# Attention and expert routing on one core: transposes as single passes, the sink columns' exponentials on their own path, transfers in halves of 64 partitions

## The chip, the cores and the metric

The kernel runs on one core of a Trainium2 chip. The metric is the device time of one execution in microseconds (us). A run is one execution; times of several runs are given by their median.

## The reference, cut to what matters

Two steps follow each other. First an attention in which every query sees the 4 first keys (the sinks) and the 128 keys up to itself; then a mixture of experts that assigns each of the 3072 tokens to one of 8 experts of equal capacity and sends it through that expert's two matrices.

```python
batch, n_heads, seq, head_dim = 4, 8, 768, 64          # n_sink, window = 4, 128
scores = (q @ k.transpose(0,1,3,2)) / sqrt(64)
keep   = (pos[None,:] < 4) | ((rel >= 0) & (rel < 128))
a      = softmax(where(keep, scores, -1e9))             # + 1e-9 in the denominator
x      = (a @ v).transpose(0,2,1,3).reshape(3072, 512)
logits = x @ w_gate                                     # 8 experts
# largest logits first, each token to one expert, at most 384 tokens per expert
out[mask] = maximum(x[mask] @ w1[e], 0) @ w2[e]         # expert by expert
```

## The kernel before, in words

The work of the attention is cut into 24 chunks: 4 batches times 6 blocks of 128 queries, all 8 heads at once. A chunk c goes through these steps; the two numbers behind a name are its two halves, four heads each.

- The loads `ldk`, `ldq` (lines 30 and 31, four chunks ahead) and `lv` (line 32) bring keys, queries and values of 256 KB each; SP issues them and the store `xo` in one order.
- `qs` (line 74, POOL) scales the queries.
- `QK0`, `QK1` (line 83, PE): scores into PSUM, as products of 64x64 parts, 8 per half. Partitions hold the queries of two 64-row parts, and the columns hold 64 keys of the block before, 4 sinks and 128 keys of the block.
- `cp`, `mx` (lines 89 to 94, DVE): masking and the negated maximum.
- `e0` to `e3` (line 99, ACT): the exponentials of 132 columns, with their sum.
- `T0`, `T1` (line 107, PE): P transposed by products with the identity, 16 per half, each 64x64. `pe` (line 108, ACT) copies them to SBUF as `PT`; `A`, `B` (lines 110 and 111, POOL) split the two diagonal parts into the keys of this block and of the one before.
- `ss` (line 114, ACT), `Ts` (line 118, PE), `pS` (line 119, ACT): the 4 sink columns of P are copied out and transposed on their own.
- `AV0`, `AV1` (line 129, PE): P times the values; `ae` (line 132, DVE) copies the result out.
- `X` (lines 136 and 138, PE): the sinks' values are added, and heads are brought into rows, 64 columns of x and 8 of the router's logits for each head; `ra`, `r` (lines 130 and 131, DVE) make one over the sum, `xe` (line 140, DVE) multiplies by it, `lm` (line 142, DVE) adds the logits up over heads.
- `xo` (line 143, SP): x to DRAM, in pieces of 64 numbers.

Products in 32-bit floats are issued to PE as two passes, each with a load of its weights of its own; so one of them appears in the trace as two MATMUL and two LDWEIGHTS instructions. A transpose in PE's transpose mode is one of each, as at line 667.

The order in which the steps of several chunks are interleaved on the five engines is computed when the kernel is built: `schedule` walks the steps with a cost for each (`table`), rings of buffers (`buffers`: four PSUM buffers `p` are shared by QK, T, Ts, AV and X), waits between engines, and a priority per step (`OFF`).

When the last chunk's logits are there, the second part starts: the routing by a search for thresholds (lines 519 to 569), the gathers of x by token (line 659), their transposes (line 667), the loads of the experts' matrices `raw`, and their products (lines 680 and 692). Its weights wait for the routing's first result.

Of the kernel before, what the change touches and what calls it, by code (L numbers as in the profile page):

```python
# [11 lines left out]
W=132  # L12
# [3 lines left out]
def attention(ctx,tc,qd,kd,vd,vs,ud,iwd,ident,idn,x_dram,L,side={}):  # L16
# [34 lines left out]
    G.memset(mf[0:64],1); G.memset(mf[64:128],0); G.memset(mf[64:128,4:8],1); G.memset(m0[0:64,0:4],1)  # L51
# [23 lines left out]
    def op_QK(c,g):  # L75

        i=c%NB; q=qs[c%NQ]; sp=T('p',c,f'QK{g}')
        k0=(i-1)*W+4 if i else -128
        for u in range(2):
            for s in range(2):  # L80
                for f in range(2):
                    p,o=half(s),half(f); a=0 if i else 64 if f else 128
                    PE.matmul(sp[o,s,196*u+a:196*u+196],q[p,g+2*u,o],kk[p,g+2*u,k0+64*f+a:k0+64*f+196],start=True,stop=True)  # L83
    def scores(c,g): return T('p',c,f'QK{g}')[:,:,0:392].rearrange("p s (u n)->p s u n",u=2)
    def op_cp(c,g):

# [26 lines left out]
    def op_ss(c):  # L113
# [16 lines left out]
    def op_ra(c): V.tensor_scalar(T('r',c),T('sm',c),1e-9,None,op0=OP.add)  # L130
# [23 lines left out]
def layouts(q,k,v,wg,n_sink=4):  # L154

    pairs=lambda x: x.reshape(B,HP,2,64,NB,-1).transpose(2,3,0,4,1,5).reshape(128,B,NB,-1)
    qT=q.transpose(0,1,3,2); kT=k.transpose(0,1,3,2)
    qd=pairs(qT.reshape(B,H,64,NB,128))
    sk=np.broadcast_to(kT[:,:,:,None,:4],(B,H,64,NB,4))
    kd=pairs(np.concatenate([sk,kT.reshape(B,H,64,NB,128)],-1))  # L160
# [12 lines left out]
    return {n:np.ascontiguousarray(a) for n,a in dict(qd=qd,kd=kd,vd=vd,vs=vs,ud=ud,iwd=iwd,ident=np.eye(128,dtype=np.float32)).items()}  # L173
# [5 lines left out]
def table(cfg):  # L179
    o={}  # L180
    def add(k,e,c,deps,alloc=()): o[k]=(e,c,deps)
# [29 lines left out]
    add('xe','V',680,[('X',0),('r',0)])  # L211
# [21 lines left out]
def schedule(cfg,off,T,nb=NC,dl={}):
# [34 lines left out]
    et=collections.defaultdict(float); et['E']=3700.0; mode=['n']; out=[]; ld=[]; fills=[]; dq=[0.0]  # L268
# [28 lines left out]
    while len(out)<total:  # L297
# [49 lines left out]
SWITCH=dict(nr=90,rn=200)  # L347
# [6 lines left out]
OFF={'A0': 18335, 'A1': 52415, 'AV0': 14908, 'AV1': 84106, 'B0': 47216, 'B1': 7783, 'QK0': 2872, 'QK1': 4297, 'T0': 8328, 'T1': -8153, 'Ts': 15650, 'U': -22652, 'Uc': -13081, 'cp0': -10470, 'cp1': 78107, 'e0': 58010, 'e1': 95573, 'e2': 687, 'e3': 927, 'fi': 95598, 'lm': -9483, 'mx0': 14597, 'mx1': -49747, 'pS': 60593, 'pe0': 61206, 'pe1': -9424, 'pr0': 95367, 'pr1': -19606, 'pr10': -47988, 'pr11': 79834, 'pr12': 60010, 'pr13': -8724, 'pr14': 3651, 'pr15': 2764, 'pr2': 75294, 'pr3': -25455, 'pr4': 59901, 'pr5': -70, 'pr6': 12471, 'pr7': 98043, 'pr8': -8311, 'pr9': 6044, 'qs': 50785, 'r': 61220, 'ra': -6513, 'ss': 79894, 'um': 11705, 'xe': -10955, 'xo': -20341, 'zs': -5463, 'pr16': -102190, 'ae': -9891, 'X': -32988}  # L354
# [374 lines left out]
def attention_general(ctx,tc,qd,kd,vd,iwd,ident,idn,x_dram,L,n_sink,window):  # L729
# [10 lines left out]
    for b in range(B):  # L740
# [6 lines left out]
        for i in range(NB):  # L747
# [74 lines left out]
```

## Time and profile before

| what | us |
|---|---|
| three runs, median (lowest to highest) | 545.25 (541.69 to 548.64) |
| the profiled execution | 545.01 |
| its span | 543.3 |

Between the span and the profiled execution's own time lie 1.7 us. In the profile PE is TensorE's matrix products and PEld its loads of weights, DVE VectorE, ACT ScalarE, POOL GpSimd, SP SyncE; SPq and PEq stand for the sequencers of these. A wait is named by what ended it; "issue" means that the engine waited for nothing that the profile shows. PEclk is the granted clock of TensorE as a share of full speed.

### The profile page before, as it was taken

To read this page: it belongs to the slowest core of one execution; us is meant where nothing else is said; L and a number is where in the kernel's file an instruction comes from. 1 tells how busy PE (TensorE), PEld (TensorE's weight loads), DVE (VectorE), ACT (ScalarE), POOL (GpSimd) and SP (SyncE) were. 2 spreads that over 40 slices of the span, in tenths; PEclk is the share of its full clock that TensorE was granted. 3 is DMA by queue.
4 is the path that set the end of the run, shared out by engine and by line. 5 is a ranking of instruction groups with operands and counts; after the bars stand their busy time and mean duration, and the time that the engine had idled before them with its cause. 6 is when DMAs were issued, how large, how long until landed. Compare 5 with 4: busy or idle time off the path is not lost.

```text
span 543.3 us, 16624 instructions
## 1 busy us (share of the span) xinstructions
PE 468.9 (86%) x6873; PEld 400.3 (74%) x6873; DVE 352.7 (65%) x1040; ACT 237.2 (44%) x690; POOL 174.0 (32%) x231
## 2 busy tenths in 40 slices
PE   7777776877777478898999998999999989999995
PEld 4666765776676246886987886887888889988983
DVE  3666656667667677789698796787798674452210
ACT  3966766776773014335253254163154244352210
POOL 6867766768543020016031021103130212001001
PEclk9999999999999569899899998999999989999999
DMA  7656645555322137056082191272290595101001
GB/s 237 201 171 167 167 140 159 160 160 167 83 74 51 32 117 246 8 187 220 21 303 85 61 326 40 74 276 79 79 329 21 180 373 184 58 21 54 25 6 53
DMA packets 75085, 73.23 MB, mean 135 GB/s; under 512 B 28033, under 2 KB 57601, under 8 KB 75009
## 3 DMA queue, kind: packets, MB, share of 16 engines
q1 hardware_dynamic: 71168, 59.58, 35.3%
q0 software_dynamic: 3840, 12.59, 6.4%
q8 instruction: 54, 0.88, 0.7%
q14 instruction: 23, 0.18, 0.1%
HBM read 59.57 MB, written 12.58 MB: 133 GB/s over the span
## 4 chain that ended last, share of the span: by engine, by line
PE 57%; DMA 15%; DVE 12%; issue 10%; ACT 2%; POOL 2%; SPq 1%; POOLq 0%; ACTq 0%; DVEq 0%
PE ph L680 16%; PE py L692 15%; DMA raw<-w 12%; PE pp L129 6%; PE pp L83 5%; PE pp L107 5%; PE pp L138 2%; PE pp L136 2%; PE pr L543 2%; DVE wl L654 2%; DVE cmp L473 2%; PE pt L667 1%; DMA xg<-x_dram,idx 1%; DVE hl L684 1%; DMA us<-ud 1%
## 5 line engine op out<-in xcount | busy, mean ns | idle before, releaser
L652 ACT ACTIVATE wh<-raw 128x1024 fp32r<-128x1024 f32 x64 | 67.8, 1060 | 76.9 <-DMA raw<-w 38.9
L680 PE MATMUL ph<-xh,wh 128*128 128x384 f32 x256 | 92.3, 360 | 4.0 <-DVE hl L684 4.0
L654 DVE TENSOR_TENSOR wl<-raw,wh 128x1024 fp32r<-128x1024 f32 x64 | 77.7, 1220 | 23.2 <-ACT wh L652 22.9
L680 PE MATMUL ph<-xl,wh 128*128 128x384 f32 x256 | 88.1, 344 | 0.0
L680 PE MATMUL ph<-xh,wl 128*128 128x384 f32 x256 | 88.0, 344 | 0.0
L692 PE MATMUL py<-wh,hh 128*128 128x512 f32 x192 | 79.9, 416 | 2.2 <-ACT yo L695 2.2
L697 POOL DMA_INDIRECT out<-yo,idx x24 | 26.7, 1114 | 166.9 <-ACT yo L695 113.4
L659 POOL DMA_INDIRECT xg<-x_dram,idx x24 | 33.3, 1389 | 139.5 <-issue 49.5
L692 PE MATMUL py<-wh,hl 128*128 128x512 f32 x192 | 75.9, 395 | 0.0
L692 PE MATMUL py<-wl,hh 128*128 128x512 f32 x192 | 75.8, 395 | 0.0
L99 ACT ACTIVATE P<-pp,nmx 128x132 f32<-128x132 f32 x192 | 69.0, 372 | 7.9 <-DVE nmx L94 6.6
L683 ACT ACTIVATE hh<-ph 128x384 fp32r<-128x384 f32 x64 | 31.2, 488 | 82.3 <-PE ph L680 61.7
L684 DVE SCALAR_TENSOR_TENSOR hl<-ph,hh 128x384 fp32r<-128x384 f32 x64 | 35.3, 553 | 39.7 <-ACT hh L683 39.1
L107 PE MATMUL pp<-idt,P 64*64 64x64 f32 x1536 | 39.6, 226 | 23.5 <-issue 23.5
L680 PEld LDWEIGHTS ph<-xh,wh 128*128 128x128 f32 x256 | 50.2, 196 | 7.1 <-DVE hl L684 5.1
L107 PEld LDWEIGHTS pp<-idt,P 64*64 64x64 f32 x1536 | 35.0, 140 | 24.0 <-issue 23.5
L110 POOL TENSOR_TENSOR E<-PT,me 128x256 f32<-128x256 f32 x48 | 35.7, 744 | 49.2 <-ACT PT L108 48.6
L680 PEld LDWEIGHTS ph<-xl,wh 128*128 128x128 f32 x256 | 49.6, 194 | 2.0
L680 PEld LDWEIGHTS ph<-xh,wl 128*128 128x128 f32 x256 | 49.6, 194 | 0.0
L83 PE MATMUL pp<-kk,q 64*64 64x196 f32 (+2 forms) x768 | 44.5, 327 | 4.8 <-issue 3.5
L108 ACT ACTIVATE PT<-pp 128x512 f32<-128x512 f32 x48 | 28.6, 597 | 33.1 <-PE pp L107 32.9
L692 PEld LDWEIGHTS py<-wh,hh 128*128 128x128 f32 x192 | 36.9, 192 | 7.6 <-ACT yo L695 2.6
(157 smaller groups left out, 863.8 us busy)
## 6 DMA issues: line engine op xcount, KB each, us to landing
raw<-w SPq DMA_DIRECT2D x64, 512.0 KB, 8.3
v<-vd SPq DMA_DIRECT2D x24, 256.0 KB, 3.8
x_dram<-xt SPq DMA_DIRECT2D x24, 256.0 KB, 3.1
kk<-kd SPq DMA_DIRECT2D x23, 264.0 KB, 4.3
q<-qd SPq DMA_DIRECT2D x23, 256.0 KB, 4.9
xg<-x_dram,idx POOLq DMA_INDIRECT x24, 5.8
out<-yo,idx POOLq DMA_INDIRECT x24, 2.8
us<-ud SPq DMA_DIRECT2D x1, 288.0 KB, 4.8
```

What stands on the lines that cost most here:

```text
L83: PE.matmul(sp[o,s,196*u+a:196*u+196],q[p,g+2*u,o],kk[p,g+2*u,k0+64*f+a:k0+64*f+196],start=True,stop=True)
L99: A.activation(T('P',c)[:,h,:],sp[:,s,u,64:196],AF.Exp,bias=T('nmx',c)[:,b:b+1],scale=1.0,accum_out=T('sm',c)[:,h:h+1])
L107: for u in range(2): PE.matmul(t[half(u),s,128*x+64*l:128*x+64*l+64],T('P',c)[half(s),2*(g+2*u)+x,a:a+64],idn[half(s),half(s)],start=True, ...
L110: def op_A(c,g): G.tensor_tensor(T('E',c)[:,2*g:2*g+2],diag(c,g),me[:,None].to_broadcast([128,2,2,64]),OP.mult)
L129: PE.matmul(av[half(s),u,a:a+64*n],T('v',c-w)[half(u),256*l+64*x:256*l+64*x+64],m.rearrange("p a n->p (a n)"),start=g==0 and n==2 and w==0 ...
L652: g.add('A',947,lambda wh=wh,raw=raw: nc.scalar.activation(wh,raw,AF.Copy),[f'raw{q}'],[f'wh{s}'],f'H{k}.{j}',f'W{k}')
L654: g.add(e,{'V':1135,'P':2303}[e],lambda wh=wh,wl=wl,raw=raw,e=e: (nc.vector if e=='V' else nc.gpsimd).tensor_tensor(wl,raw,wh.bitcast(F32) ...
L659: g.add('P',1038,lambda t=t: nc.gpsimd.indirect_dma_start(out=self.xg[t],out_offset=None,in_=self.x_dram,in_offset=bass.IndirectOffsetOnAx ...
L680: nc.tensor.matmul(p[:,0:CAP],x[:,c,:],y[:,c,:],start=c==0 and i==0,stop=c==3 and i==2)
L683: g.add('A',371,lambda f=f,p=p: nc.scalar.activation(self.hh[:,f,:],p[:,0:CAP],AF.Relu),ps,[f'hh{f}'],f'hh{k}.{f}',f'H{k}')
L684: g.add('V',469,lambda f=f,p=p: nc.vector.scalar_tensor_tensor(self.hl[:,f,:],p[:,0:CAP],0.0,self.hh[:,f,:].bitcast(F32),op0=OP.max,op1=OP ...
L692: nc.tensor.matmul(p,x[:,f,ts],w,start=f==0 and i==0,stop=f==7 and i==2)
```

## The change

1. **Transposes in one pass.** P is stored as [4 pairs][2 halves of keys][2 heads][64], so that 64 rows by 128 columns can be transposed at once in PE's transpose mode; T is 8 such instructions per half in place of 16 products of 64x64, and Ts is 2 in place of 4. The weights' part is 64x128 where every other product of the attention keeps its 64x64.
2. **The sinks apart.** The keys are stored with the sinks ahead of each 64 keys (`W` 136 for 132), scores have 200 columns in place of 196, and the exponentials of P cover 128 keys without the sinks. A new DVE step `sd` subtracts the maximum from the sinks' scores, `ss` takes their exponentials in one ACT instruction in place of two copies, a new DVE step `rs` adds them up, and `ra` adds this to the other sum.
3. **x in 2 KB rows.** `xe` writes 512 columns of x and 64 of logits as two instructions, and `xo` sends rows of 512 numbers.
4. **Transfers in halves.** Loads of queries and keys from chunk 4 on, of values from chunk 1 on, and all stores are issued as two transfers of 64 partitions.
5. **The planner** has new costs for these steps, a cost for each change between kinds of PE instructions, a term for every 256th PE instruction, and a new table of priorities.

```diff
-W=132
+W=136
+    def move(a,b,whole=0):
+        for p in (slice(0,128),) if whole else (half(0),half(1)): nc.sync.dma_start(a[p],b[p])
...
-            A.activation(T('P',c)[:,h,:],sp[:,s,u,64:196],AF.Exp,bias=T('nmx',c)[:,b:b+1],scale=1.0,accum_out=T('sm',c)[:,h:h+1])
+            A.activation(T('P',c)[:,2*g+s,:,u,:],sp[:,s,u,64:200].rearrange("p (a n)->p a n",a=2)[:,:,4:68],AF.Exp,bias=T('nmx',c)[:,b:b+1],scale=1.0,accum_out=T('sm',c)[:,h:h+1])
+    def op_sd(c,g):
+        V.tensor_tensor(T('sd',c)[:,:,g::2,:],scores(c,g)[:,:,:,132:136],nmx(c,g)[:,:,:,None].to_broadcast([128,2,2,4]),OP.add)
...
-                    a=((68,0),(4,68))[s][l]
-                    for u in range(2): PE.matmul(t[half(u),s,128*x+64*l:128*x+64*l+64],T('P',c)[half(s),2*(g+2*u)+x,a:a+64],idn[half(s),half(s)],start=True,stop=True)
+                    PE.transpose(t[:,s,128*x+64*l:128*x+64*l+64],T('P',c)[half(s),2*g+x,1-(l^s)].rearrange("p u n->p (u n)"),idn[half(s),half(s)])
...
-        for f,a in ((0,64),(1,0)): A.activation(ss(c)[half(f),:,c//NB],T('P',c)[half(f),:,a:a+4].rearrange("p (h s) k->p s h k",s=2),AF.Copy)
+    def op_ss(c): A.activation(ss(c)[:,:,c//NB],T('sd',c),AF.Exp)
...
-            for r in range(2): PE.matmul(t[half(r),s,0:64],x[half(s),half(r)],idn[half(s),half(s)],start=True,stop=True)
+            PE.transpose(t[:,s,0:64],x[half(s)],idn[half(s),half(s)])
...
+    def op_rs(c): V.tensor_reduce(T('r',c).rearrange("p (j s)->p s j",s=2),ss(c)[:,:,c//NB],AX.X,OP.add)
+    def op_ra(c): V.scalar_tensor_tensor(T('r',c),T('r',c),1e-9,T('sm',c),op0=OP.add,op1=OP.add)
...
+        for a,b,n in ((0,64,0),(64,72,512)):
+            V.tensor_tensor(T('xt',c)[:,n:n+8*(b-a)].rearrange("p (j s n)->p s j n",s=2,j=4),x[:,:,:,a:b],r.to_broadcast([128,2,4,b-a]),OP.mult)
...
-    def op_xo(c): nc.sync.dma_start(x_dram[c*128:(c+1)*128,:].rearrange("p (h d)->p h d",h=H),T('xt',c)[:,:,0:64])
+    def op_xo(c): move(x_dram[c*128:(c+1)*128,:],T('xt',c)[:,0:512])
...
-    b['p']=(4,{**{f'QK{h}':[f'e{2*h}',f'e{2*h+1}'] for h in range(2)},...
+    b['p']=(4,{**{f'QK{h}':[f'e{2*h}',f'e{2*h+1}',f'sd{h}'] for h in range(2)},...
```

The order of PE, the kernel before, in the middle of the first batch. One row is one product or a run of equal ones (as many as its x says); L83 is QK, L107 T, L118 Ts, L129 AV, L136 and L138 X.

```order
L107 MATMUL pp_215<-idt,P_245 64x64 x16
L107 MATMUL pp_214<-idt,P_245 64x64 x16
L83 MATMUL pp_216<-kk,q_165 64x196 x8
L129 MATMUL pp_215<-PT_256,v_242 64x128 x4
L129 MATMUL pp_215<-PT_256,v_243 64x128 x4
L129 MATMUL pp_215<-E_259,v_243 64x64 x4
L129 MATMUL pp_215<-E_259,v_242 64x64 x4
L118 MATMUL pp_214<-idt,ss_2_226 64x64 x4
```

The order of PE, the changed kernel, some chunk later, where a row for each step of a chunk follows the other; L84 is QK, L111 T, L121 Ts, L132 AV, L140 and L142 X.

```order
L132 MATMUL pp_213<-E_262,v_242 64x64 x4
L111 MATMUL pp_215<-idt,P_246 128x64 x8
L84 MATMUL pp_214<-kk,q_166 64x200 x8
L111 MATMUL pp_216<-idt,P_246 128x64 x8
L121 MATMUL pp_215<-idt,ss_2_226 128x64 x2
L84 MATMUL pp_213<-kk,q_166 64x200 x8
L140 MATMUL pp_215<-vx,pS_266 64x288 x4
L142 MATMUL pp_215<-iw,at_273 64x72 x16
L132 MATMUL pp_216<-PT_260,v_241 64x128 x4
```

Transposes stood in two runs of 16 and a run of 4 between products of the same shape; now they are two runs of 8, the second with Ts behind it, each between products of another shape, so that PE changes its shape four times a chunk.

The order of SP, the kernel before, one chunk: the store of x, then values, keys and queries. DMAHW0 to DMAHW7 are the names of the semaphores that transfers count up when they have landed; a transfer takes the next of the eight in turn, and waits for the last transfer that had it.

```order
L143 DMA x_dram<-xt_273 1024x1x64 [waits DMAHW0_49,DVE_49]
L32 DMA v_243<-vd 128x512 [waits DMAHW1_49,PE_49]
L31 DMA kk<-kd 128x4x132 [waits DMAHW2_49,PE_49]
L30 DMA q_166<-qd 128x512 [waits DMAHW3_49,Pool_49]
```

The order of SP, the changed kernel, one chunk (line 31 is now the helper that all of them go through):

```order
L31 DMA x_dram<-xt_276 64x512 [waits DMAHW7_49,DVE_49]
L31 DMA x_dram<-xt_276 64x512 [waits DMAHW0_49]
L31 DMA kk<-kd 64x4x136 [waits DMAHW1_49,PE_49]
L31 DMA kk<-kd 64x4x136 [waits DMAHW2_49,PE_49]
L31 DMA q_166<-qd 64x512 [waits DMAHW3_49,Pool_49]
L31 DMA q_166<-qd 64x512 [waits DMAHW4_49]
L31 DMA v_242<-vd 64x512 [waits DMAHW5_49,PE_49]
L31 DMA v_242<-vd 64x512 [waits DMAHW6_49,PE_49]
```

A chunk has eight transfers in place of four, and so a transfer waits for one that was issued one chunk earlier, where it was two.

In the second part of the kernel the order of PE, ACT, POOL and SP is the same in both; on DVE seven small steps of the routing's preparation stand a few places earlier or later.

## Rows read from the trace of the kernel before

**Rows 1.** The busy time by stretch: from the start to the first `xe`, from there to the last `xe`, and from the routing to the end. Columns: us, then busy us and (instructions) of each engine, granted clock, DMA share, GB/s.

```profile
0.00:23.00 23.00, 17.87 (x345) 12.01 (x346) 11.01 (x27) 13.08 (x58) 16.46 (x62) 0.93 0.77 238
23.00:175.30 152.30, 113.74 (x4543) 103.79 (x4543) 99.48 (x227) 101.67 (x450) 97.43 (x123) 0.99 0.50 136
...
178.00:543.30 365.30, 336.31 (x1974) 283.68 (x1974) 239.56 (x775) 122.50 (x184) 60.06 (x48) 0.95 0.37 128
```

**Rows 2.** The instructions of line 140 (`xe`), one for each chunk: shortest, median and longest in ns, first and last start in us.

```profile
L140 DVE TENSOR_TENSOR xt<-pp,r x24: 735/752/759, 23.0 to 175.3; 128x576 f32<-128x576 f32 x24
```

**Rows 3.** PE's waits from 23.0 to 175.3: who waited for what, us in total, times, longest.

```profile
PE pp L107 <- issue: 22.6, 16, 2.2
PE pp L138 <- issue: 5.4, 4, 1.9
PE pp L129 <- issue: 4.6, 8, 1.2
PE pp L83 <- issue: 3.5, 3, 2.3
```

**Rows 4.** PE's matmuls in order of time from one such wait to the next: start, us to the end of the last of them, what, how many; in brackets the idle time before.

```profile
44.86 0.48 PE L138 MATMUL pp<-iw,at 64*64 64x72 f32 x17 [1.43 <-issue]
...
45.18 0.63 PE L107 MATMUL pp<-idt,P 64*64 64x64 f32 x30
...
45.64 0.67 PE L83 MATMUL pp<-kk,q 64*64 64x132 f32 x15
46.29 0.67 PE L129 MATMUL pp<-PT,v 64*64 64x128 f32 x16
...
46.98 0.32 PE L118 MATMUL pp<-idt,ss 64*64 64x64 f32 x8
47.10 0.65 PE L129 MATMUL pp<-PT,v 64*64 64x128 f32 x16
47.54 0.32 PE L129 MATMUL pp<-E,v 64*64 64x64 f32 x6
48.51 0.29 PE L129 MATMUL pp<-E,v 64*64 64x64 f32 x4 [0.65 <-issue]
```

**Rows 5.** The DMA queue of that name from 0 to 180 us: packets, MB, share of 16 engines.

```profile
q8 instruction: 38, 0.62, 1.4%
```

**Rows 6.** The stretch from one issue wait's end to the next, for the longest that was read, the one of rows 4, and the shortest; columns as in rows 1.

```profile
66.26:71.62 5.36, 3.49 (x127) 3.30 (x127) 3.25 (x7) 3.38 (x16) 3.46 (x5) 1.00 0.74 202
44.85:48.50 3.65, 2.99 (x128) 2.65 (x127) 2.95 (x6) 1.60 (x7) 3.30 (x5) 1.00 0.31 68
79.94:83.45 3.51, 2.95 (x127) 2.71 (x127) 2.65 (x5) 2.33 (x11) 1.81 (x4) 1.00 0.32 70
```

**Rows 7.** Groups of instructions by line, from 23.0 to 175.3: how many, busy us, mean ns of one, and the idle time before them.

```profile
L107 PE MATMUL pp<-idt,P 64*64 64x64 f32 x1407 | 36.0, 222 | 22.6 <-issue 22.6
...
L118 PE MATMUL pp<-idt,ss 64*64 64x64 f32 x184 | 8.8, 222 | 1.5 <-ACT P L99 0.9 <-issue 0.7
...
L131 DVE RECIPROCAL r<-r 128x8 f32<-128x8 f32 x22 | 4.4, 198 | 0.5
```

**Rows 8.** The chain of waits, in the second part: start, us, and six transposes of 128x128 in PE's transpose mode in one piece of it.

```profile
295.03 0.70 PE pt L667 x6
```

**Rows 9.** PE's matmuls in the first 14 us, where products of 128x128 weights and of 64x64 weights follow each other.

```profile
0.84 3.15 PE L55 MATMUL pp<-const-float32-0.0 128*128 128x512 bf16 x7 [0.84 <-PEq L815]
3.92 1.37 PE L83 MATMUL pp<-kk,q 64*64 64x68 f32 x16
...
10.56 1.06 PE L69 MATMUL pp<-us 128*128 128x8 f32 x8 [1.64 <-DMA us<-ud]
11.55 1.39 PE L83 MATMUL pp<-kk,q 64*64 64x196 f32 x16
```

**Rows 10.** POOL in order of time, a chunk without a pause (`A` and `B` twice, then the scaling of queries).

```profile
25.23 0.73 POOL L110 TENSOR_TENSOR E<-PT,me 128x256 f32<-128x256 f32 x1 [0.41 <-ACT PT L108]
26.04 0.73 POOL L111 TENSOR_TENSOR PT<-PT,mi 128x256 f32<-128x256 f32 x1
...
28.22 1.49 POOL L74 TENSOR_SCALAR q<-q 128x512 f32<-128x512 f32 x1
```

**Rows 11.** SP's issues of one chunk, in order of time: start, us of the issue.

```profile
39.18 0.53 SPq L143 DMA_DIRECT2D x_dram<-xt  x1
39.80 0.62 SPq L32 DMA_DIRECT2D v<-vd  x1
40.51 0.44 SPq L31 DMA_DIRECT2D kk<-kd  x1
41.04 0.52 SPq L30 DMA_DIRECT2D q<-qd  x1
```

**Rows 12.** Stretches with a lower granted clock, and one with transposes of line 667 in it; columns as in rows 1.

```profile
95.00:97.00 2.00, 2.00 (x68) 1.93 (x64) 1.06 (x3) 0.95 (x5) 1.08 (x2) 0.50 0.00 0
...
178.00:194.00 16.00, 7.49 (x54) 3.67 (x55) 10.43 (x59) 0.00 (x0) 0.00 (x0) 0.53 0.03 7
204.00:206.00 2.00, 1.78 (x21) 1.43 (x19) 1.51 (x8) 0.00 (x0) 0.00 (x0) 1.00 0.43 129
```

**Rows 13.** The DMA queue that moves the data, from 175.9 to 179.5 us, while the last two stores of x land.

```profile
q1 hardware_dynamic: 2080, 0.52, 65.4%
```

More of the change, by code (lines that the diff above doesn't have):

```diff
@@ L81, in op_QK, with scores @@
                 for f in range(2):
-                    p,o=half(s),half(f); a=0 if i else 64 if f else 128
-                    PE.matmul(sp[o,s,196*u+a:196*u+196],q[p,g+2*u,o],kk[p,g+2*u,k0+64*f+a:k0+64*f+196],start=True,stop=True)
-    def scores(c,g): return T('p',c,f'QK{g}')[:,:,0:392].rearrange("p s (u n)->p s u n",u=2)
+                    p,o=half(s),half(f); a=0 if i else 68 if f else 132; k0=(i-1)*W+4+68*f
+                    PE.matmul(sp[o,s,200*u+a:200*u+200],q[p,g+2*u,o],kk[p,g+2*u,k0+a:k0+200],start=True,stop=True)
+    def scores(c,g): return T('p',c,f'QK{g}')[:,:,0:400].rearrange("p s (u n)->p s u n",u=2)
     def op_cp(c,g):
@@ L159, in layouts @@
     sk=np.broadcast_to(kT[:,:,:,None,:4],(B,H,64,NB,4))
-    kd=pairs(np.concatenate([sk,kT.reshape(B,H,64,NB,128)],-1))
+    kb=kT.reshape(B,H,64,NB,2,64)
+    kd=pairs(np.concatenate([sk,kb[:,:,:,:,0],sk,kb[:,:,:,:,1]],-1))
     vd=v.reshape(B,2,4,NB,2,64,64).transpose(1,5,0,3,4,2,6).reshape(128,B,NB,512)
@@ L186, in table @@
     for h in range(2):
-        add(f'QK{h}','E',lambda c: 660 if c%NB else 445,[('ldk',0),('ldk',-1),('qs',0)]+[(f'{n}{x}',0) for x in ((0,1),(2,))[h] for n in ('qs.','ldk')])
+        add(f'QK{h}','E',lambda c: 675 if c%NB else 445,[('ldk',0),('ldk',-1),('qs',0)]+[(f'{n}{x}',0) for x in ((0,1),(2,))[h] for n in ('qs.','ldk')])
         add(f'cp{h}','V',lambda c: 335 if c%NB>1 else 490 if c%NB else 670,[(f'QK{h}',0)])
         add(f'mx{h}','V',615,[(f'cp{h}',0)])
-        for u in range(2): add(f'e{2*h+u}','A',697,[(f'mx{h}',0)])
+        add(f'sd{h}','V',95,[(f'mx{h}',0)])
+        for u in range(2): add(f'e{2*h+u}','A',690,[(f'mx{h}',0)])
     ae=[(f'e{h}',0) for h in range(4)]
     for g in range(2):
-        add(f'T{g}','E',490,[(f'e{2*g}',0),(f'e{2*g+1}',0),('ldn',0)])
+        add(f'T{g}','E',250,[(f'e{2*g}',0),(f'e{2*g+1}',0),('ldn',0)])
         add(f'pe{g}','A',479,[(f'T{g}',0)])
@@ L197, in table @@
     add('zs','P',lambda c: 480 if c%NB==1 and c//NB<B-1 else None,[('B1',0)])
-    add('ss','A',260,ae+[('~zs',1-NB)])
-    add('ra','V',75,ae)
+    add('ss','A',140,[('sd0',0),('sd1',0)]+[('~zs',1-NB)])
+    add('rs','V',100,[('ss',0)])
+    add('ra','V',75,ae+[('rs',0)])
     add('r','V',120,[('ra',0)])
-    add('Ts','E',130,[('ss',0),('ldn',0)])
+    add('Ts','E',65,[('ss',0),('ldn',0)])
     add('pS','A',230,[('Ts',0)])
@@ L210, in table @@
     add('X','E',980,[('ae',0),('pS',0),('um',0),('ldi',0)])
-    add('xe','V',680,[('X',0),('r',0)])
+    add('xe','V',740,[('X',0),('r',0)])
     add('lm','V',135,[('xe',0)])
@@ L321, in schedule @@
             if e=='E':
-                md='n' if k=='U' else 'r'
-                t1+=SWITCH.get(mode[0]+md,0); mode[0]=md
+                md='n' if k=='U' else 't' if k[0]=='T' else 'r'
+                t1+=SWITCH.get(mode[0]+md,0); mode[0]=md; ins[0]+=INS[k]//(2 if k[:2]=='AV' and c%NB==0 else 1)
+                if ins[0]>=256:
+                    w=max(0,ins[1]+FETCH-(t1-cost*(ins[0]-256)/INS[k])); t1+=w; ins[1]=t1-cost*(ins[0]-256)/INS[k]; ins[0]-=256
             if e=='E' and s<60000 and s-et[e]>400:
@@ L346 @@
 SOLO={'p'}
-SWITCH=dict(nr=90,rn=200)
+SWITCH=dict(nr=90,rn=200,nt=90,tn=200,rt=100,tr=200)
+INS=dict(QK0=32,QK1=32,T0=16,T1=16,Ts=4,AV0=64,AV1=64,X=80,U=16); FETCH=3900
 def plan_of(res,cfg):
@@ L764, in attention_general @@
                     sp=ps.tile([128,384],F32,name="sp",bufs=2)
-                    nc.tensor.matmul(sp,q[hs,h//2,:],kT[hs,h//2,3*g:3*g+3,4:W],start=True,stop=True)
+                    nc.tensor.matmul(sp,q[hs,h//2,:],kT[hs,h//2,3*g:3*g+3].rearrange("p b (l w)->p b l w",l=2)[:,:,:,4:68],start=True,stop=True)
                     nc.scalar.activation(sc[:,384*g:384*g+384],sp,AF.Copy,scale=0.125)
```

45 lines of the change are left out of this document (21 added, 24 removed).

## The prediction

> **What bounds the kernel now.** I began with the stretches [rows 1]. The second part, from the routing on, takes 365.3 us and the change leaves its PE order alone, so what matters is the attention. Its first `xe` starts at 23.0 and its last at 175.3 us [rows 2]: 23 chunk intervals in 152.3 us, 6.62 us each. In that stretch no engine is full: of 152.3 us PE is busy 113.7, ACT 101.7, DVE 99.5, POOL 97.4, and the DMA share is 0.50 [rows 1].
>
> PE's waits say why [rows 3]. Nearly all of PE's idle time is "issue": 22.6 + 5.4 + 4.6 + 3.5 = 36.1 us in 31 times. It waits for no other engine there. Read one stretch between two such waits [rows 4]: PE runs through parts of X, T, QK, AV, Ts and AV without a pause, and stops in the middle of a run of equal products. From one wait's end to the next there are 128 matmuls in one stretch and 127 in two others, as the edges were cut, each with its load of weights [rows 6]: 256 instructions. The queue named "instruction" moved 38 packets and 0.62 MB up to 180 us [rows 5], 16 KB a packet. So I read these waits as PE running dry: its instructions come in blocks of 256, and the next block isn't there yet. The 4543 matmuls of the stretch [rows 1] are 35.5 blocks; 152.3 / 35.5 = 4.29 us for a block. A block takes longer where data moves beside it: 3.51 us at a DMA share of 0.32, 3.65 at 0.31, 5.36 at 0.74 [rows 6]. PE's work and its other, small waits without the issue waits are 152.3 - 36.1 = 116.2 us, 5.05 us a chunk. So the attention is bound by the supply of PE's instructions.
>
> [...]
>
> **The change part by part.**
>
> *Transposes, the supply side.* In the stretch T has 1407 matmuls and Ts 184 [rows 7]. T's 16 products of two passes become 8 instructions of one pass, and Ts's 4 become 2: a quarter each, 352 and 46. That leaves 4543 - 1055 - 138 = 3350 matmuls, 26.2 blocks, 1.139 a chunk. At 4.29 us a block the supply needs 4.88 us a chunk in place of 6.62. The same bytes now pass in less time, so the DMA share rises; against that stands the lighter store (below). I keep the whole spread seen, 3.5 to 5.4 us a block.
>
> *Transposes, PE's own time.* T takes 45.17 to 45.64, 0.47 us per half now [rows 4]. The nearest row for the new form is six 128x128 transposes in 0.70 us, 0.117 us each [rows 8]. Eight of those would be 0.94 us per half, the upper bound. The new ones move half the columns (64), and the two 64-row halves can stand side by side in the array as the four quarters do now, so the lower bound is a quarter of it, 0.235. I take 0.25, nearest to what the four quarters do now: a chunk saves 2 x (0.47 - 0.25) = 0.44 us, or at worst pays 0.94. Ts goes from 0.12 (46.98 to 47.10) to half, another -0.06. QK gets 200 columns for 196: 2% of 2 x 0.65 us, +0.03.
>
> *Changes of shape.* The trace has no 64x128 products between 64x64 ones; the nearest are changes between 128x128 and 64x64 [rows 9]. There the next product starts 0.07 us before the modelled end of the last one (0.84 + 3.15 against 3.92; 10.56 + 1.06 against 11.55), where within one shape it starts 0.17 us before (45.18 + 0.63 against 45.64 [rows 4]). So a change costs about 0.1 us; I take 0.13, with bounds of 0 and 0.25 (a whole matmul's length, 222 ns [rows 7], and a little). Four a chunk: +0.5 us, 0 to 1.0. PE's own time is then 5.05 - 0.44 - 0.06 + 0.03 + 0.5 = 5.08 us a chunk, between 4.58 and 6.96.
>
> *The sinks apart.* ACT has one `ss` less a chunk. DVE gets four small instructions more (two `sd`, `rs`, the second piece of `xe`), at about 0.2 us of busy time each as `r` has it, 198 ns [rows 7], less where they overlap: +0.4 to +0.8 us on 99.5 / 23 = 4.33 us a chunk, so DVE comes to 4.7 to 5.1. `sd` also holds QK's PSUM buffers, but the four exponentials of the same half hold them longer, so I cost it at nothing; it loses that cover if DVE falls behind. On the chain of a chunk, `ss`, Ts and `pS` now start after `sd` and no longer after the last exponential, which takes a wait away from X.
>
> *x in 2 KB rows.* The last two stores kept 65.4% of 16 engines busy for 3.6 us [rows 13]: 2.35 us, 1.18 us a store, with 2080 packets. Nothing waits for a store but its buffer. I take 0 for it on the path; it makes room for the instruction packets.
>
> *Halves.* SP issues a chunk's four transfers in 0.53 + 0.62 + 0.44 + 0.52 = 2.1 us [rows 11]. Eight half-size ones cost between 2.1 (by rows) and 4.2 us (by transfer), below a chunk's 5.4 either way. Keys and queries come four chunks ahead. Values are the tight ones: issued at QK0 and needed at AV0, with SP's order and the transfer one chunk earlier (the semaphore's last user) ahead of them. I take 0, with +0.7 us a chunk as the upper bound (2.1 us more of issue, a third of it on the path).
>
> *Together.* PE now has two limits of one size: 5.08 us a chunk of its own, which is 5.08 / 1.139 = 4.46 us per block, and a supply of 3.5 to 5.4 us per block. Spread evenly, the later of the two is 4.46 + 0.94² / (2 x 1.9) = 4.69 us on average, 5.34 us a chunk. POOL needs 28.22 + 1.49 - 25.23 = 4.48 us a chunk [rows 10] and DVE up to 5.1, so I add 0.06 for their late buffers: 5.4 us. Against the profiled execution, 545.0 us: 23 x (6.62 - 5.4) = 28.1 us go, 516.9 us are left. That execution lies 0.2 us below the median of the three runs, so it stands for them. Start and second part are taken as unchanged; the routing waits for the last chunk and moves with it.
>
> **The rivals.**
>
> *Crossings are hidden, nothing is gained.* If the issue waits are not a matter of instruction count, the stretch keeps 6.62 + 0.03 us: 546 us. Against it stand the 256 instructions between two waits, which fit to one. Chance 0.04.
>
> *The next engines hold it.* DVE at 5.1 us a chunk, POOL at 4.48 and four PSUM buffers, or values that land late, leave PE waiting 0.7 us a chunk: 6.1 us, 533 us. For it: PE has hardly waited for others so far because it was the slowest. Against it: the steps work two to three chunks apart. Chance 0.17, of which 0.05 lie within 2%.
>
> *The supply gets light.* If lighter stores and halves bring blocks to the fast end, 3.51 us, and shape changes cost nothing, PE needs 4.58, supply 4.0, and POOL's 4.48 with its own pauses decides: 4.85 us, 504 us. Chance 0.14.
>
> *Slower: PE's clock falls.* [...] If transposes keep the clock up less than the products that they replace, part of a chunk runs at half speed. With a share f of PE's 5.08 us at half clock a chunk takes 5.4 + 5.08 f; from f = 0.24 the kernel is slower than before, and at f = 0.5 it takes 7.94 us a chunk, 575 us. Against it: the issue waits get shorter, and the transposes of line 667 run at 1.00 from 204 to 206 us [rows 12]. [...] Chance 0.05.
>
> **How the numbers follow.** The forecast, 517 us, has 0.60, and its own range is 508 to 526 (5.0 to 5.8 us a chunk). A measurement here tells 2% from no change, 534.3 to 556.2 us. Faster: 0.60 + 0.14 + 0.12 = 0.86. Same: 0.05 + 0.04 = 0.09. Slower: 0.05. The range goes from the light supply to just past the rival of the next engines, 503 to 535; about 0.17 is left out.
>
> **What would show it.** After the change: 23 intervals of `xe` in about 124 us; about 26 blocks there, still 128 load-and-matmul pairs long, with issue waits in total below 12 us; T below 0.3 us per half; granted clock 0.99; the stretch behind the last `xe` 368 us as before. I am wrong if the issue waits go and PE waits for POOL, DVE or values by as much; if T or its neighbours are stretched; if the clock falls; or if the second part changes its length by more than a few us.

## The result

The changed kernel takes 524.93 us, the median of 4 runs (521.94 to 527.13), against 546.19 us (541.69 to 548.64) for the kernel before: a ratio of 0.962, with a 95% interval of 0.954 to 0.970. It is faster by 3.8%. The time lies in the predicted range, 8 us above the forecast of 517. Two runs took twice the usual time (1,096 us, the kernel before, and 1,098 us, the kernel with products and whole transfers below); they count in the medians and not in the ratios.

The profiled execution took 521.94 us, with a span of 520.2 us. The first, second and last stretch of the changed kernel answer to [rows 1]; the one from 131 to 135 us is read further down. Columns: us, then busy us and (instructions) of PE, PE's weight loads, DVE, ACT and POOL, granted clock, DMA share, GB/s.

```profile
0.00:23.00 23.00, 16.62 (x262) 10.02 (x266) 12.57 (x37) 13.49 (x59) 17.33 (x61) 1.00 0.82 229
23.00:158.10 135.10, 113.91 (x3338) 93.23 (x3330) 105.32 (x314) 93.62 (x424) 95.84 (x123) 0.96 0.59 155
...
131.00:135.00 4.00, 4.00 (x88) 2.98 (x86) 2.65 (x9) 2.19 (x10) 1.45 (x2) 0.66 0.51 124
...
161.00:520.20 359.20, 332.66 (x1971) 279.98 (x1970) 238.54 (x768) 122.75 (x184) 61.72 (x48) 0.96 0.37 129
```

The attention, from the first `xe` to the last, has gone from 152.3 to 135.1 us: 5.87 us a chunk where it was 6.62. That is 17.2 us. (The last `xe` counted here is the second, small piece, 0.6 us behind the large one; it adds 0.03 us a chunk to every version with two pieces.) What lies behind the last `xe` has gone from 368.0 to 362.1 us, another 5.9 us, and the edits don't reach there (see below).

The `xe` of the changed kernel, now two instructions a chunk, stands against [rows 2].

```profile
L146 DVE TENSOR_TENSOR xt<-pp,r x48: 209/447/692, 23.0 to 158.1; 128x512 f32<-128x512 f32 x24, 128x64 f32<-128x64 f32 x24
```

The waits of all engines in that stretch stand against [rows 3]: who waited for what, us in total, times, longest.

```profile
ACT P L104 <- DVE sd L99: 17.9, 34, 1.9
POOL E L114 <- ACT PT L112: 17.2, 9, 3.1
POOL q L76 <- DMA q<-qd: 12.7, 8, 3.8
...
DVE xt L146 <- DMA x_dram<-xt: 7.7, 4, 3.2
...
PE pp L111 <- DVE sd L99: 6.5, 5, 2.1
...
PE pp L84 <- DVE xt L146: 5.4, 3, 2.9
...
PE pp L111 <- ACT P L104: 3.9, 12, 0.9
...
PE pp L121 <- DVE at L136: 1.7, 1, 1.7
```

The 36.1 us in which PE waited for "issue" are gone: PE itself has no such row left. In their place PE waits 19.3 us for other engines, in the rows shown and some smaller ones. Two rows are new: POOL waits 12.7 us for queries that haven't landed, and DVE waits 7.7 us until the store of x has freed the buffer that `xe` wants to write.

How such a wait comes about is seen in order of time (start, us to the end of the last of them, engine, what, how many; in brackets the idle time before), first on SP, then on DVE and PE.

```profile
120.99 1.19 SPq L31 DMA_DIRECT2D q<-qd  x2
122.27 1.18 SPq L31 DMA_DIRECT2D x_dram<-xt  x2
123.55 2.23 SPq L31 DMA_DIRECT2D v<-vd  x2
125.87 1.19 SPq L31 DMA_DIRECT2D x_dram<-xt  x2
127.16 1.18 SPq L31 DMA_DIRECT2D v<-vd  x2
...
103.53 0.82 DVE L146 TENSOR_TENSOR xt<-pp,r 128x512 f32<-128x512 f32 x2 [2.18 <-DMA x_dram<-xt]
104.27 0.16 DVE L99 TENSOR_TENSOR sd<-pp,nmx 128x16 f32<-128x16 f32 x1
...
129.03 0.82 DVE L146 TENSOR_TENSOR xt<-pp,r 128x512 f32<-128x512 f32 x2 [3.25 <-DMA x_dram<-xt]
...
104.50 0.47 PE L111 MATMUL pp<-idt,P 64*128 64x64 f32 x8 [2.14 <-DVE sd L99]
...
129.91 1.48 PE L84 MATMUL pp<-kk,q 64*64 64x200 f32 x16 [2.91 <-DVE xt L146]
```

From 121 to 128 us SP goes from one issue to the next with pauses of 0.1 us. The store at 125.87 is issued by 127.06, and a half of a store lands 2.5 us after its issue (the median), which fits with the `xe` that starts at 129.03. PE stands 2.91 us behind it. The rows from 103.5 us on show a second way: `xe` is late for the same reason, `sd` stands behind it on DVE, and T waits until `sd` has let go of a PSUM buffer. From 131 to 135 us PE is busy throughout, but at a granted clock of 0.66 (in the first fence): read in steps of half a microsecond it is 0.50 from 130.5 to 133.5 us, 0.79 in the next step and 1.00 from 134.0 us on. The 16 matmuls of `QK` that start at 129.91 take 1.48 us; at the full clock such a run takes 0.91 (the rows of "The transposes themselves" below).

SP's issues, from the view of their line (count: shortest, median, longest issue in ns; first and last start), stand against [rows 11].

```profile
L31 SPq DMA_DIRECT2D x_dram<-xt x48: 445/587/1602, 25.7 to 158.9; - x48
L31 SPq DMA_DIRECT2D v<-vd x47: 430/547/2015, 6.2 to 143.0; - x47
L31 SPq DMA_DIRECT2D kk<-kd x46: 402/644/1905, 0.8 to 120.3; - x46
L31 SPq DMA_DIRECT2D q<-qd x46: 421/570/1515, 1.3 to 121.6; - x46
```

A half takes 0.59 us to issue, about as long as a whole transfer took before. So eight of them take 4.7 us a chunk at the median, and some take far longer (up to 2.0 us): SP is at issuing for 105.5 of the 135.1 us, for 154 transfers, 0.69 us each on average. (Expectations below say 113.8 us, and 36.9 for whole transfers; the issues in the traces add up to less, 105.5 and 33.8.) From 39 to 128 us it issues for 79.4 of 89 us; but for one of 0.4 us, its pauses there are 0.1 us.

### The profile page after: what moved, and what is told of

It is laid out like the page before. It is cut to its first block, busy times and chain, and to the rows that moved or that the text cites. A ratio compares the mean times of both kernels' runs of the same rounds, so it can differ in the third digit from the quotient of the medians.

```text
span 520.2 us, 14348 instructions
## 1 busy us (share of the span) xinstructions
PE 464.5 (89%) x5577; PEld 384.3 (74%) x5577; DVE 359.0 (69%) x1136; ACT 229.9 (44%) x666; POOL 174.9 (34%) x231
## 3 DMA queue, kind: packets, MB, share of 16 engines
q1 hardware_dynamic: 51056, 59.79, 37.9%
## 4 chain that ended last, share of the span: by engine, by line
PE 42%; DVE 22%; DMA 18%; ACT 10%; issue 4%; POOL 2%; SPq 1%; POOLq 0%; DVEq 0%; ACTq 0%
PE ph L691 16%; PE py L703 15%; DMA raw<-w 11%; ACT P L104 7%; DMA x_dram<-xt 3%; DMA xg<-x_dram,idx 3%; PE pp L84 3%; PE pr L554 3%; DVE nmx L96 2%; DVE cmp L484 2%; PE pt L678 2%; DVE xt L146 1%; ACT wh L663 1%; PE pp L111 1%; DVE hl L695 1%
## 5 line engine op out<-in xcount | busy, mean ns | idle before, releaser
L691 PE MATMUL ph<-xh,wh 128*128 128x384 f32 x256 | 91.0, 356 | 2.6 <-DVE hl L695 2.6
L691 PE MATMUL ph<-xh,wl 128*128 128x384 f32 x256 | 86.8, 339 | 0.0
L691 PE MATMUL ph<-xl,wh 128*128 128x384 f32 x256 | 86.6, 338 | 0.0
L670 POOL DMA_INDIRECT xg<-x_dram,idx x24 | 34.6, 1440 | 137.9 <-issue 49.7
L104 ACT ACTIVATE P<-pp,nmx 128x128 f32<-128x128 f32 x192 | 68.2, 369 | 21.3 <-DVE sd L99 18.6
L695 DVE SCALAR_TENSOR_TENSOR hl<-ph,hh 128x384 fp32r<-128x384 f32 x64 | 35.2, 552 | 38.4 <-ACT hh L694 37.8
L84 PE MATMUL pp<-kk,q 64*64 64x200 f32 (+2 forms) x768 | 44.2, 338 | 7.3 <-DVE xt L146 5.4
L691 PEld LDWEIGHTS ph<-xh,wl 128*128 128x128 f32 x256 | 48.5, 189 | 0.0
L703 PEld LDWEIGHTS py<-wh,hl 128*128 128x128 f32 x192 | 36.0, 188 | 8.1
L76 POOL TENSOR_SCALAR q<-q 128x512 f32<-128x512 f32 x23 | 34.5, 1500 | 16.5 <-DMA q<-qd 16.5
L706 ACT ACTIVATE yo<-py 128x512 f32<-128x512 f32 x24 | 14.3, 596 | 57.9 <-PE py L703 36.6
```

The lines of the kernel that those rows point to most:

```text
L76: def op_qs(c,h=slice(0,HP),e=G): e.tensor_scalar(qs[c%NQ][:,h],qs[c%NQ][:,h],0.125,None,op0=OP.mult)
L84: PE.matmul(sp[o,s,200*u+a:200*u+200],q[p,g+2*u,o],kk[p,g+2*u,k0+a:k0+200],start=True,stop=True)
L104: A.activation(T('P',c)[:,2*g+s,:,u,:],sp[:,s,u,64:200].rearrange("p (a n)->p a n",a=2)[:,:,4:68],AF.Exp,bias=T('nmx',c)[:,b:b+1],scale=1. ...
L670: g.add('P',1038,lambda t=t: nc.gpsimd.indirect_dma_start(out=self.xg[t],out_offset=None,in_=self.x_dram,in_offset=bass.IndirectOffsetOnAx ...
L691: nc.tensor.matmul(p[:,0:CAP],x[:,c,:],y[:,c,:],start=c==0 and i==0,stop=c==3 and i==2)
L695: g.add('V',469,lambda f=f,p=p: nc.vector.scalar_tensor_tensor(self.hl[:,f,:],p[:,0:CAP],0.0,self.hh[:,f,:].bitcast(F32),op0=OP.max,op1=OP ...
```

## The experiments

All times are medians, each ratio is to the kernel before on the same chip and has its 95% interval. An interval per chunk is 1/23 of the time from the first `xe` to the last of the profiled execution. Beside the first four experiments the kernel before itself took 540.74 to 551.08 us, so small differences are read from the stretches and not from the ratios.

**Whole transfers, all else as changed.** Is it the halves that keep the chunk at 5.87 us?

```diff
-for p in (slice(0,128),) if whole else (half(0),half(1)): nc.sync.dma_start(a[p],b[p])
+for p in (slice(0,128),): nc.sync.dma_start(a[p],b[p])
```

> The changed kernel with every transfer whole (128 partitions, four a chunk). The changed kernel takes 5.87 us a chunk between its first and last xe, 135.1 us in all. Theory A, SP's issuing is the limit (half transfers take about 0.6 us each to issue, eight a chunk, so 4.8 us, and loads and stores land late): the interval falls to 5.5 us or less, POOL's wait for queries (12.7 us) and xe's wait for its store (7.7 us) fall below a third, the total is 512 to 518 us. Theory B, the engines' own work on a chunk is the limit: 5.8 to 5.9 us, 522 to 526 us. Theory C, the halves are what lets PE's instruction blocks through: issue waits of 10 us or more come back, 6.1 us or more, 528 us or more.

Measured: 516.73 us (512.28 to 517.78), 0.941 [0.931, 0.952]; 5.33 us a chunk. The stretch of the attention in the columns of the first fence:

```profile
24.30:147.00 122.70, 110.44 (x3338) 89.77 (x3330) 105.05 (x312) 93.21 (x424) 96.31 (x123) 1.00 0.53 164
```

Its SP issues, one transfer each:

```profile
L31 SPq DMA_DIRECT2D kk<-kd x26: 378/412/1222, 0.8 to 105.4; - x26
L31 SPq DMA_DIRECT2D q<-qd x26: 328/458/670, 1.3 to 106.0; - x26
L31 SPq DMA_DIRECT2D v<-vd x24: 328/383/1901, 6.1 to 130.6; - x24
L31 SPq DMA_DIRECT2D x_dram<-xt x24: 320/326/327, 25.0 to 147.1; - x24
```

Its waits in the stretch:

```profile
ACT P L104 <- DVE sd L99: 13.3, 35, 1.0
...
PE pp L111 <- ACT P L104: 6.0, 15, 0.9
...
POOL q L76 <- DMA q<-qd: 0.8, 2, 0.6
PE pp L132 <- issue: 0.6, 1, 0.6
...
PE pp L84 <- issue: 0.5, 2, 0.3
```

SP is at issuing for 33.8 us in place of 105.5, for 75 transfers. The wait for queries has shrunk from 12.7 to 0.8 us, `xe` waits for no store any more, and the granted clock is 1.00. The halves cost 135.1 - 122.7 = 12.4 us of the stretch, 0.54 us a chunk, and 8.2 us between the medians; behind the last `xe` the profiled execution is 7.0 us longer here (369.1 against 362.1). PE's own rows say how: its waits add up to 19.3 us with halves and 10.5 with whole transfers, and it is busy 113.9 against 110.4 us with the same 3338 matmuls, as the clock is at 1.00 and not 0.96. That is 8.8 + 3.5 = 12.3 of the 12.4 us. PE's waits for `sd` fall from 6.5 to 0.9 us.

**Another buffer for x.** The planner gives `xt` the buffer that came free last, which is the one whose store is still under way. Here it takes the one that has been free longest, with halves as in the changed kernel.

```diff
-while j+1<len(f) and f[j+1][0]<=s: j+=1
+while t!='xt' and j+1<len(f) and f[j+1][0]<=s: j+=1
```

> The changed kernel, but xe takes the buffer that has been free the longest, where it took the one freed last; order and transfers are the same. Theory A (the store lands later than the planner thinks, because SP issues it late, and xe runs into it): xe's wait for its store falls from 7.7 us to below 1 us, the interval from 5.87 to 5.6 or 5.8 us a chunk, since SP stays the limit: 518 to 523 us. Theory B: the wait only moves to another place, 5.87 us, 522 to 526 us.

Measured: 523.74 us (521.73 to 525.79), 0.956 [0.946, 0.967]; 5.73 us a chunk. `xe` waits for no store any more, but POOL's wait for queries grows from 12.7 to 19.6 us. PE's AV now waits 8.3 us for POOL, a wait that the changed kernel doesn't have. So the waits move and the gain is small, too small to tell from none (the interval is in the range of A, the total in that of B): the buffer was only one place at which SP's lateness came out.

**Whole transfers and the other buffer.** Both edits together.

> The changed kernel with whole transfers and with xe taking the buffer that has been free the longest. Theory A: both late causes go, 5.2 to 5.4 us a chunk, 510 to 515 us. Theory B: no better than the changed kernel, 522 to 526 us. Theory C: issue waits as in the first of these runs, 528 us or more.

Measured: 516.26 us (514.66 to 520.84), 0.942 [0.933, 0.951]; 5.53 us a chunk, which none of the three had. Of its PE waits 4.2 us are issue waits, where whole transfers alone had 1.1. Nothing is seen that the buffer gives once SP is on time.

**Products put back in place of the transposes.** Is it the number of PE's instructions that counted? The transposes become pairs of products again, as many as before; halves and all else stay as changed.

```diff
-PE.transpose(t[:,s,128*x+64*l:...],T('P',c)[half(s),2*g+x,1-(l^s)]...,idn[half(s),half(s)])
+[PE.matmul(t[half(u),s,128*x+64*l:...],T('P',c)[half(s),2*g+x,1-(l^s),u],idn[half(s),half(s)],start=True,stop=True) for u in range(2)]
...
-PE.transpose(t[:,s,0:64],x[half(s)],idn[half(s),half(s)])
+[PE.matmul(t[half(r),s,0:64],x[half(s),half(r)],idn[half(s),half(s)],start=True,stop=True) for r in range(2)]
```

> The changed kernel with T and Ts as products of 64x64 again (16 and 4 of two passes each), everything else as changed. Theory A of the prediction (PE's instruction blocks set the pace): the stretch between first and last xe has about 35 blocks again, issue waits of 30 us or more, 6.5 us a chunk or more, 537 to 546 us. Rival (the old waits came from the old order, not from the count of instructions): issue waits stay below 10 us, at most 6.0 us a chunk, 522 to 529 us.

Measured: 537.02 us (534.52 to 540.92), 0.982 [0.970, 0.994]; 6.47 us a chunk, with 4508 matmuls in the stretch. PE's waits of the stretch:

```profile
PE pp L84 <- issue: 7.0, 6, 1.4
PE pp L132 <- issue: 7.0, 9, 1.5
PE pp L111 <- issue: 6.9, 6, 2.4
PE pp L142 <- issue: 4.7, 6, 1.4
PE pp L121 <- issue: 2.4, 2, 1.4
PE pp L140 <- issue: 1.9, 3, 0.8
```

The issue waits are back, 29.9 us in 32, and they stand before whatever line happens to cross into the next block: from one to the next the trace has 126 or 127 matmuls, or twice that. The edit puts back the mode and the shape of the transposes along with their number; the even distance says that the number is what counts. The order of the steps and the other edits stayed as changed, so they don't remove these waits.

**Products and whole transfers.** Do the halves speed up or slow down PE's instruction blocks? Products as just shown, transfers whole.

> Whole transfers, and T and Ts as products of 64x64 (the run before it with halves and products took 6.47 us a chunk, 27 us of issue waits, 537 us). It tells whether halves let PE's instruction blocks through faster. If they do: blocks take longer here, 6.6 us a chunk or more, issue waits of 32 us or more, 539 to 546 us. If they only cost SP's time, which is hidden at this pace: 6.4 to 6.5 us, 534 to 539 us.

Measured: 540.58 us (538.42 to 542.49, but for the one of 1,098), 0.994 [0.990, 0.997]; 6.46 us a chunk, with 29.6 us of issue waits in 28. With 4512 matmuls that is 35.2 blocks of 4.22 us. So halves or whole makes no difference to the supply (6.47 and 6.46), and the 12.4 us that the halves cost are seen only once the supply has stopped being the bound. It also says what the new order, the sinks' own path and the rows of 2 KB are worth without the one-pass transposes: 6.46 us a chunk against 6.62.

**SP kept busy by itself.** Whole transfers, with two small loads of 64 partitions (16 bytes each, into a buffer that nobody reads) behind each of them: 12 issues a chunk, with next to no more bytes.

```diff
-for p in (slice(0,128),) if whole else (half(0),half(1)): nc.sync.dma_start(a[p],b[p])
+nc.sync.dma_start(a,b)
+for _ in range(0 if whole else 2):
+    nc.sync.dma_start(junk[jn[0]%8],kd[0:64,0,0,0:4]); jn[0]+=1
```

> Whole transfers as in the first run (5.33 us a chunk, SP issues for 36.9 of 122.7 us), and behind each of them two loads of 64 partitions by 16 bytes into tiles that nobody reads. Theory A (SP's issue time was what the halves cost): at 0.45 to 0.6 us each these bring SP to 5.2 to 6.5 us a chunk, it issues without a pause, and the interval follows it: 5.8 us or more, POOL's wait for queries is back at 8 us or more, 523 us or more. Theory B (the halves cost something in the transfers themselves: landing, engines, bytes): hardly any bytes are added, 5.3 to 5.5 us a chunk, 515 to 519 us.

Measured: 562.52 us (562.18 to 563.06), 1.031 [1.023, 1.038]: slower than the kernel before. 7.47 us a chunk; the stretch:

```profile
23.80:195.50 171.70, 125.30 (x3338) 100.09 (x3330) 107.80 (x312) 94.58 (x424) 95.89 (x123) 0.84 0.47 125
```

Its SP in order of time:

```profile
62.07 1.11 SPq L34 DMA_DIRECT2D junk<-kd  x2
63.28 0.53 SPq L32 DMA_DIRECT2D v<-vd  x1
63.85 1.10 SPq L34 DMA_DIRECT2D junk<-kd  x2
65.06 0.53 SPq L32 DMA_DIRECT2D x_dram<-xt  x1
```

The DMA share is the lowest of the versions with one-pass transposes (0.47) and the interval the longest, so it is the issuing that binds and not the moving of bytes: SP issues for 144.8 of the 171.7 us. At 6.3 us a chunk that is inside Theory A's 5.2 to 6.5; the interval is longer still. POOL waits 31.7 us for queries and `xe` 38.3 us for its store, and PE, at a clock of 0.84, is busy 125.3 us with the work that takes 110.4 at 1.00. A small load costs as much to issue as half a transfer, 0.59 us at the median; and a whole transfer between them takes 0.53 us here, where it took 0.33 to 0.38 in the first experiment.

**Two transfers by columns.** As many transfers as in the changed kernel, but each of all 128 partitions and half the columns.

```diff
-for p in (slice(0,128),) if whole else (half(0),half(1)): nc.sync.dma_start(a[p],b[p])
+n=a.shape[1]
+for p in (slice(0,n),) if whole else (slice(0,n//2),slice(n//2,n)): nc.sync.dma_start(a[:,p],b[:,p])
```

> The changed kernel with each transfer split in two by columns (128 partitions, half of each row) and not by partitions: eight transfers a chunk, all with half the bytes, as in the changed kernel. If the issue costs a fixed time per transfer, SP is as full as in the changed kernel (113.8 of 135.1 us): 5.8 us a chunk, 522 to 527 us. If the form with 64 partitions is what is slow to issue (0.59 us median where a whole store takes 0.33), SP is at 3 us a chunk and the interval near that of whole transfers: 5.3 to 5.5 us, 514 to 519 us.

Measured: 512.44 us (510.56 to 515.37), 0.940 [0.933, 0.948]; 5.34 us a chunk. Its issues:

```profile
L32 SPq DMA_DIRECT2D x_dram<-xt x48: 319/422/1736, 24.5 to 147.0; - x48
L32 SPq DMA_DIRECT2D v<-vd x47: 359/422/2647, 6.2 to 131.4; - x47
L32 SPq DMA_DIRECT2D kk<-kd x46: 378/426/1492, 0.8 to 106.8; - x46
L32 SPq DMA_DIRECT2D q<-qd x46: 340/420/1707, 1.3 to 107.9; - x46
```

With 0.42 us in place of 0.59 at the median, 0.54 in place of 0.69 on average, eight issues a chunk cost the interval nothing: POOL waits 3.9 us for queries, `xe` 0.5 us for a store, and the granted clock is 1.00. SP issues for 81.6 of the 122.8 us. So neither the number of transfers nor that of packets does the harm (59,632 packets in the data queue of this kernel, 51,056 in the changed one), but the form: 64 partitions. A transfer waits for the one that was issued eight before it in both, so that isn't it either. Slow issues aren't confined to it: whole loads took 0.44 to 0.62 us in the kernel before [rows 11], where the store goes in 256-byte pieces. Why some issues are slow stays open.

**x in 256-byte pieces again.** Whole transfers, with `xt`, `xe` and the store of x as in the kernel before (pieces of 64 columns for each head).

> Whole transfers, and x as before: xe in one instruction, rows of 72 in its buffer, the store in pieces of 64 numbers. If the lighter store makes room for the instruction blocks or the loads: 0.1 to 0.3 us a chunk slower than with whole rows (5.33), 518 to 524 us. If the store was hidden, as the prediction has it: 5.25 to 5.4 us a chunk, 514 to 519 us.

Measured: 513.99 us (512.00 to 516.81), 0.941 [0.934, 0.949]; 5.44 us a chunk, against 5.33 with rows of 2 KB. The store takes 0.52 us to issue again. 0.1 us a chunk is all that the 2 KB rows can claim, and the whole time shows none of it. PE's issue waits are 4.3 us here against 1.1; but with 2 KB rows and the other buffer they were 4.2, so the store isn't shown to be their cause.

No version is told apart from the others among whole transfers, columns and 256-byte pieces (ratios of 0.940 to 0.942); all of them beat the changed kernel, whose interval begins at 0.954 where theirs end at 0.952 or lower, and whose stretch is 135.1 us where theirs are 122.7 to 125.2.

## Why the prediction was right where it was, and where it wasn't

*The bound.* It held. PE was held up by the supply of its instructions in blocks of 256, as I read the 127 or 128 matmuls, each with its load, from one wait to the next [rows 6]. With a quarter of the attention's matmuls gone the waits at the crossings, from one such block into the next, went from 36.1 us (36.8 with the 0.7 of [rows 7], left out of the sum) to none on PE; with the products put back they came back, with halves (29.9 us) and without (29.6 us). The forecast said less than 12 us of them. The queue named "instruction" moved 44 packets over the whole of the changed kernel, and 54 over the kernel before and where the products are back, where the counts per stretch differ by 9 blocks (4543 and 4508 against 3338 matmuls):

```profile
q8 instruction: 44, 0.72, 0.6%
```

*The crossings.* PE waits at them in the three kernels that go through a block in 4.2 to 4.3 us: 36.1 us in the kernel before, 29.9 and 29.6 us with the products. With the transposes and whole transfers, 122.7 us for 3338 / 128 = 26.1 blocks are 4.70 us each, and 1.1 us of issue waits are left. But they don't end at one pace: with 256-byte pieces (4.80 us a block) 4.3 us of them are left, and with the other buffer (4.88) 4.2.

*The transposes themselves.* PE in one chunk of the kernel with whole transfers, at a clock of 1.00, in order of time, stands against [rows 4]:

```profile
92.80 0.46 PE L111 MATMUL pp<-idt,P 64*128 64x64 f32 x8
93.19 0.91 PE L84 MATMUL pp<-kk,q 64*64 64x200 f32 x16
94.03 0.46 PE L111 MATMUL pp<-idt,P 64*128 64x64 f32 x8
94.33 0.23 PE L121 MATMUL pp<-idt,ss 64*128 64x64 f32 x2
94.49 0.91 PE L84 MATMUL pp<-kk,q 64*64 64x200 f32 x16
95.22 0.66 PE L140 MATMUL pp<-vx,pS 64*64 64x288 f32 x8
```

From start to start, T takes 0.30 us where Ts, of the same shape, follows, and 0.39 where `QK` does: a change of shape costs 0.09. `QK` takes 0.73 us where X follows and 0.84 where T does: 0.11. So T takes 0.30 us where 0.47 stood and 0.25 was forecast, and a change costs about 0.1 where 0.13 was forecast; both lie within their bounds. Added up, T, Ts and `QK` take 0.39 + 0.84 + 0.30 + 0.16 + 0.73 = 2.42 us here, with three of a chunk's four changes of shape, where [rows 4] have 2 x (0.47 + 0.65) + 0.12 = 2.36. So these rows show no saving of PE's own time by the transposes, as the sum had it (-0.44 - 0.06 + 0.03 + 0.5 = +0.03): what they bring is fewer instructions. PE's busy time is 110.4 / 23 = 4.80 us a chunk, below the 113.7 / 23 + 0.03 = 4.97 of the sum; what makes it lower stays open.

*The interval of 5.4 us.* It came out for the kernel with whole transfers, 5.33 us and 516.7 us against 5.4 and 517. But its parts are other ones: the supply adds 1.1 / 23 = 0.05 us and not 0.26, and PE's waits for ACT's exponentials and other engines 0.41 us (10.5 us less the 1.1 of issue, over 23) and not the 0.06 that I gave them with the 0.10 of small waits that stand in the 5.05. A part of the agreement is luck. So is a part of the whole time's: by the interval alone the profiled execution would have come out 23 x (5.87 - 5.4) = 10.8 us above 517; it lies 5 us above, because 5.9 us went behind the last `xe`, where no edit reaches.

*The halves.* This step failed. I had put eight issues at "between 2.1 (by rows) and 4.2 us (by transfer), below a chunk's 5.4 either way", and taken 0 with 0.7 us as the upper bound. They measure 4.7 us at the median, and SP issues for 79.4 of 89 us on end. Issuing that fills nine tenths of the time wasn't hidden here; loads and stores started late, and what depends on them was late. A second term that had been put at nothing went with it: `sd` was said to hold PSUM buffers no longer than the exponentials unless DVE falls behind; with `xe` late it does fall behind, and PE waits 6.5 us for `sd` (0.9 with whole transfers). The cost is 0.54 us a chunk, 12.4 us of the 135.1. That is nearly the 0.5 us by which 5.87 exceeds the forecast of 5.4.

*x in 2 KB rows.* Right within what its experiment can tell: 0 on the path, to 0.1 us a chunk.

*DVE.* 105.3 us in place of 99.5, which is 0.25 us a chunk more where 0.4 to 0.8 were forecast. It is not the bound.

*The clock.* I had 0.99 and a rival in which the transposes lower it; its half clock is the 0.50 of [rows 12], which the kernel before shows from 94 to 97 us, behind an issue wait of 2.06 us that ends at 93.64 (one of 2.27 us that ends at 88.56 leaves it at 1.00). It stands at 1.00 with whole transfers and the same transposes, and at 0.96 in the changed kernel, where it falls behind long waits of PE (to 0.50 from 107 to 109 us, behind one of 2.14 us that ends at 104.50, and to 0.50 from 130.5 us on, behind the one of 2.91 us; though not behind each: after the wait of 2.4 us that ends at 56.0 it stays at 1.00). So the transposes didn't lower it.

*The rest of the kernel.* 368 us were forecast, 362.1 are measured. With the same PE order the eight experiments have 362.3 to 369.1 us there, without relation to their edits (the two kernels with products 362.4 and 365.7, whole transfers 369.1, columns 362.3). What makes it vary was not pursued. So of the 23.1 us between the two profiles the attention's 17.2 are what the change is shown to do, and the other 5.9 stay without a cause.

*The rivals.* "Crossings are hidden", "the supply gets light" and "PE's clock falls" have not come. "The next engines hold it" is what came in part, by late queries and stores (it had named values), at 5.87 us where it was priced at 6.1.

## What to carry to other kernels

Where PE pauses in the middle of equal products and the trace names no other engine, count the instructions between two pauses; if they are the same number each time, try fewer instructions first: here 3338 matmuls in place of 4543 took these waits from 36.1 us to none, and transfers in halves or whole made no difference to them (29.9 and 29.6 us with the products). When that bound goes, add up what every other queue needs in the new, shorter interval, with the issue time for each form of transfer. Here a queue that issued for 105.5 of 135.1 us set the pace, and one that issued for 81.6 of 122.8 us did not. Don't cut a transfer by partitions for nothing: here one transfer of 128 partitions, or two by columns, cost less to issue (0.33 to 0.46 us, or two of 0.42, against two of 0.59).

## What the runs showed that I had not expected

- A transfer of 64 partitions takes longer to issue (0.59 us) than the whole transfer of 128 (0.33 to 0.46 us), and than one of 128 partitions with half the columns (0.42 us). A load of 16 bytes for each of 64 partitions takes 0.59 us. A whole transfer between such loads takes 0.53 us.
- T, Ts and `QK` take PE no less time with one-pass transposes than with products (2.42 against 2.36 us): each change of shape read cost 0.09 or 0.11 us.
- The store of x takes 0.33 us to issue as rows of 2 KB and 0.52 us as pieces of 256 bytes, with the same bytes.
- One wait of 2.9 us on PE cost more than itself: from 1.1 to 5.1 us after its end, the granted clock was 0.66. Over the stretch of the changed kernel this is 3.5 us of PE's busy time, and 14.9 us (125.3 against 110.4) in the kernel with the small loads.
